# Block-sparse attention and a token/channel mixer: hand-emitted program order against an order made by a list scheduler

## The chip, the cores and the metric

The kernel runs on one core of one Trainium2 chip. The metric is the time of one execution on the device, in microseconds (us). Lower is better. The engines are named as in the profile: PE is TensorE, DVE is VectorE, ACT is ScalarE, POOL is GpSimd, SP is SyncE.

## What is computed

Attention over 4 batches of 8 heads, 768 positions and 64 elements a head, with a mask made of blocks of 32, and behind it a mixer over tokens and channels. Cut to what matters:

```python
scores = q @ k.transpose(0, 1, 3, 2) / np.sqrt(D)      # (4, 8, 768, 768)
mask = band of blocks | first and last block row and column | 3 sampled blocks per block row
attn = softmax(np.where(mask, scores, -1e9))
x = (attn @ v).transpose(0, 2, 1, 3).reshape(4, 768, 512)
h = np.maximum(x.transpose(0, 2, 1) @ w_tok1, 0.0) @ w_tok2   # 768 -> 256 -> 768
u = x + h.transpose(0, 2, 1)
out = u + np.maximum(u @ w_ch1, 0.0) @ w_ch2                  # 512 -> 1536 -> 512
```

## The kernel before

Work goes head by head, 32 slots in all. For a slot, `load_qkv` (L132 to L134) loads q, k and v through POOL's queue, position p of each block of 128 on partition p, so that every partition gets six separate runs of 64 elements. `emit_transposes` turns the six blocks of q (L188) and of k (L196) on PE, one head at a time, and DVE copies the results (L193, L201) into `qtb` and `ktb`. These have 24 more rows, which hold the mask in a form that the score matmul adds by itself: `indf` says to which block a position belongs, `e2sb` which blocks are forbidden. They are built at the start on POOL, DVE and PE (L82 to L174) and put in place by four loads within SBUF (L177, L178).

`attention` then goes through six blocks of 128 keys, called steps here. A step makes the scores of 128 keys against 768 queries (L214 with 512 columns, L218 with 256) in one of two `ps` buffers; ACT takes the exp of all 768 into `et` (L222); six matmuls of 65 columns (L224, called PV here) add into `po`, whose 65th column collects the sums. After six steps DVE takes the reciprocals (L232) and scales the six blocks into `x` (L234).

`make_mixer_groups` cuts the mixer of a batch into 38 groups: two for the first token matmuls (`g_tok1`, L249), six for the second, the addition of x and the transposes of u (`g_tok2`, L268, L276, L279, L284), 24 for the first channel matmuls and their relu (`g_ch1`, L296, relu on DVE at L302), six for the second and the output (`g_ch2`, L313, L320, L321). They share two psum buffers `pm`.

The order of every engine comes from the order in which the code calls these functions, and from priorities: transposes, scores and the scaling stand in `high_priority` blocks, PV and mixer behind them. The groups of a batch are handed out over the seven slots that follow it by `PACING`; the last batch's groups come when all slots are done.

Of the kernel before, what the change touches and what calls it, by code (L numbers as in the profile page):

```python
# [23 lines left out]


@with_exitstack
def kernel(
# [12 lines left out]
    nc = tc.nc  # L40
# [5 lines left out]
    NSLOT = B * H  # L46
    MASKVAL = -30000.0
    NSRC = 4
# [5 lines left out]
    psM = ctx.enter_context(tc.tile_pool(name="psM", bufs=2, space=bass.MemoryType.PSUM))  # L54

    qsrc = [sb1.tile([128, NC, 64], BF16, name=f"qsrc{n}") for n in range(NSRC)]
    ksrc = [sb1.tile([128, NC, 64], BF16, name=f"ksrc{n}") for n in range(NSRC)]
    vaug = [sb1.tile([128, NC, 65], BF16, name=f"vaug{n}") for n in range(NSRC)]

    qtb = [sb1.tile([128, S], BF16, name=f"qtb{i}") for i in range(2)]  # L60
    ktb = [sb1.tile([128, S], BF16, name=f"ktb{i}") for i in range(2)]

    w_tok1 = sb1.tile([128, 6, 256], BF16, name="w_tok1")
    w_tok2 = sb1.tile([128, 2, 768], BF16, name="w_tok2")
    w_ch1 = sb1.tile([128, 4, 1536], BF16, name="w_ch1")
    w_ch2 = sb1.tile([128, 12, 512], BF16, name="w_ch2")

    ident = sb1.tile([128, 128], BF16, name="ident")

    samp64 = sb1.tile([24, 3], I64, name="samp64")  # L70
    sampf = sb1.tile([24, 6], FP32, name="sampf")
    kbi = sb1.tile([24, 24], I32, name="kbi")
    kbf = sb1.tile([24, 24], FP32, name="kbf")
    eq0 = sb1.tile([24, 24], FP32, name="eq0")
    eq1 = sb1.tile([24, 24], FP32, name="eq1")
    allow = sb1.tile([24, 24], FP32, name="allow")
    bandg = sb1.tile([24, 24], FP32, name="bandg")
    t2add = sb1.tile([24, 24], BF16, name="t2add")
    indf = sb1.tile([24, S], BF16, name="indf")
    e2sb = sb1.tile([24, S], BF16, name="e2sb")  # L80

    nc.gpsimd.memset(ident[:, :], 1.0)  # L82
# [4 lines left out]
    nc.gpsimd.iota(kbi[:, :], pattern=[[1, 24]], base=0, channel_multiplier=0)  # L87
    nc.gpsimd.memset(bandg[:, :], 1.0)
    nc.gpsimd.affine_select(
        out=bandg[:, :], in_=bandg[:, :], compare_op=ALU.is_ge, fill=0.0,  # L90
        base=1, pattern=[[1, 24]], channel_multiplier=-1,
    )
    nc.gpsimd.affine_select(
        out=bandg[:, :], in_=bandg[:, :], compare_op=ALU.is_ge, fill=0.0,
        base=1, pattern=[[-1, 24]], channel_multiplier=1,
    )
    nc.gpsimd.affine_select(
        out=bandg[:, :], in_=bandg[:, :], compare_op=ALU.is_ge, fill=1.0,
        base=-1, pattern=[[0, 24]], channel_multiplier=1,
    )  # L100
# [12 lines left out]
    nc.gpsimd.memset(indf[:, :], 1.0)
    nc.gpsimd.affine_select(
        out=indf[:, :], in_=indf[:, :], compare_op=ALU.is_ge, fill=0.0,
        base=0, pattern=[[1, S]], channel_multiplier=-32,
    )
    nc.gpsimd.affine_select(
        out=indf[:, :], in_=indf[:, :], compare_op=ALU.is_ge, fill=0.0,
        base=31, pattern=[[-1, S]], channel_multiplier=32,  # L120
    )

    def qkv_src_ap(t: bass.AP, b: int, h: int) -> bass.AP:
        off = (b * H + h) * S * D
        return APx(t, off, [[D, 128], [128 * D, NC], [1, D]])

    def load_qkv(slot):
        if slot >= NSLOT:
            return
        b, h = slot // H, slot % H  # L130
        n = slot % NSRC
        nc.gpsimd.dma_start(out=ksrc[n][:, :, :], in_=qkv_src_ap(k, b, h))  # L132
        nc.gpsimd.dma_start(out=qsrc[n][:, :, :], in_=qkv_src_ap(q, b, h))  # L133
        nc.gpsimd.dma_start(out=vaug[n][:, :, 0:64], in_=qkv_src_ap(v, b, h))  # L134

    load_qkv(0)
# [42 lines left out]
    for n in range(NSRC):  # L179
        nc.vector.memset(vaug[n][:, :, 64:65], 1.0)  # L180
# [221 lines left out]
```

## Time and profile before

| what | before |
|---|---|
| time, median of 3 runs | 361.43 us (360.75 to 367.4) |
| profiled execution, span | 362.9 us |
| PE busy | 325.2 us, 90% |
| DVE busy | 182.1 us, 50% |
| ACT busy | 142.1 us, 39% |
| POOL busy | 89.7 us, 25% |
| chain that ended last | PE 76%, ACT 8%, DMA 8%, POOL 3%, DVE 2% |

The profile is of one execution. Its span, from the first to the last instruction, is 1.5 us above the median of the runs, 0.4%; the profile shows no time outside the span. A matmul's duration in the profile goes to the end of its last result, and matmuls overlap in the engine, so that the spacing of starts in a run without gaps says what one costs. The granted clock is given as a share of TensorE's full 2.4 GHz: 1.00 is 2.4 GHz, 0.50 is 1.2 GHz, and values between are means over a stretch.

### The profile page before, as it was taken

To read this page: it belongs to the slowest core of one execution; us is meant where nothing else is said; L and a number is where in the kernel's file an instruction comes from. 1 tells how busy PE (TensorE), PEld (TensorE's weight loads), DVE (VectorE), ACT (ScalarE), POOL (GpSimd) and SP (SyncE) were. 2 spreads that over 40 slices of the span, in tenths; PEclk is the share of its full clock that TensorE was granted. 3 is DMA by queue.
4 is the path that set the end of the run, shared out by engine and by line. 5 is a ranking of instruction groups with operands and counts; after the bars stand their busy time and mean duration, and the time that the engine had idled before them with its cause. 6 is when DMAs were issued, how large, how long until landed. Compare 5 with 4: busy or idle time off the path is not lost.

```text
span 362.9 us, 6617 instructions
## 1 busy us (share of the span) xinstructions
PE 325.2 (90%) x2786; PEld 183.3 (51%) x2786; DVE 182.1 (50%) x478; ACT 142.1 (39%) x193; POOL 89.7 (25%) x123
## 2 busy tenths in 40 slices
PE   0795688899899999999999999999999999679995
PEld 0453356565556555455555555455555555235542
DVE  3331243436768633356667544347676534546722
ACT  1293467775622334465604333385404440000000
POOL 9954543524310222233210222220000000000000
PEclk9997599999999999999999999999999999859999
DMA  5999959688641455559531565651101012000022
GB/s 40 136 198 194 153 37 67 46 54 53 41 29 8 28 62 85 84 61 60 33 23 11 34 88 84 75 51 12 13 0 13 2 58 98 21 0 2 0 85 90
DMA packets 82162, 20.24 MB, mean 56 GB/s; under 512 B 75892, under 2 KB 78548, under 8 KB 82132
## 3 DMA queue, kind: packets, MB, share of 16 engines
q0 software_dynamic: 78496, 13.38, 47.3%
q1 hardware_dynamic: 3636, 6.44, 4.7%
q8 instruction: 22, 0.36, 0.4%
q14 instruction: 8, 0.07, 0.1%
HBM read 26.74 MB, written 6.29 MB: 91 GB/s over the span
## 4 chain that ended last, share of the span: by engine, by line
PE 76%; ACT 8%; DMA 8%; POOL 3%; DVE 2%; issue 2%; ACTq 0%; POOLq 0%
PE pm_ch L296 19%; PE pm_ch L313 16%; PE ps L214 13%; PE po L224 10%; ACT et L222 8%; PE ps L218 5%; PE tk L196 4%; DMA w_ch<-in_moe_w_ch_dram 3%; PE pm_tok L249 3%; PE tq L188 3%; PE pm_tok L268 3%; DMA qsrc<-in_q_dram 3%; DMA w_tok<-in_moe_w_tok_dram 2%; PE pm_ut L279 2%; DVE u L276 1%
## 5 line engine op out<-in xcount | busy, mean ns | idle before, releaser
L222 ACT ACTIVATE et<-ps 128x768 bf16<-128x768 f32 x192 | 140.8, 814 | 155.2 <-PE po L224 132.6
L214 PE MATMUL ps<-qtb,ktb 88*128 88x512 bf16 x192 | 76.3, 397 | 7.8 <-ACT et L222 6.4
L296 PE MATMUL pm_ch<-uT,w_ch 128*128 128x384 bf16 x384 | 75.0, 332 | 0.0
L313 PE MATMUL pm_ch<-w_ch,rc 128*128 128x512 bf16 x288 | 71.4, 379 | 0.0
L302 DVE TENSOR_SCALAR rc<-pm_ch 128x384 bf16<-128x384 f32 x96 | 53.1, 556 | 18.3 <-PE pm_ch L296 14.3
L224 PEld LDWEIGHTS <-et 128*128 128x128 bf16 x1152 | 50.7, 100 | 18.0 <-issue 2.8
L224 PE MATMUL po<-vaug,et 128*128 128x65 bf16 x1152 | 58.2, 196 | 0.0
L218 PE MATMUL ps<-qtb,ktb 88*128 88x256 bf16 x192 | 54.2, 282 | 0.0
L132 POOL DMA_DIRECT2D ksrc<-in_k_dram x32 | 26.7, 833 | 96.1 <-PE tk L196 86.0
L296 PEld LDWEIGHTS <-w_ch 128*128 128x128 bf16 x384 | 36.7, 99 | 27.1 <-issue 4.2
L193 DVE COPY qtb<-tq 64x768 bf16<-64x768 bf16 x32 | 17.6, 549 | 61.3 <-PE ps L218 59.7
L134 POOL DMA_DIRECT2D vaug<-in_v_dram x32 | 26.5, 829 | 77.6 <-PE po L224 74.3
L313 PEld LDWEIGHTS <-rc 128*128 128x128 bf16 x288 | 26.5, 97 | 27.5
L234 DVE TENSOR_SCALAR x<-po,recip 128x64 bf16<-128x64 f32 x192 | 39.7, 276 | 1.0
L320 DVE TENSOR_TENSOR o<-pm_ch,u 128x512 f32<-128x512 f32 x24 | 16.5, 687 | 38.7 <-PE pm_ch L313 38.7
L201 DVE COPY ktb<-tk 64x768 bf16<-64x768 bf16 x32 | 17.6, 549 | 34.6 <-PE tk L196 32.5
L218 PEld LDWEIGHTS <-ktb 88*128 88x128 bf16 x192 | 19.0, 99 | 27.3 <-issue 19.3
L133 POOL DMA_DIRECT2D qsrc<-in_q_dram x32 | 26.6, 831 | 8.5 <-PE tq L188 7.8
L214 PEld LDWEIGHTS <-ktb 88*128 88x128 bf16 x192 | 19.0, 99 | 14.1 <-issue 2.8
L188 PE MATMUL tq<-ident,qsrc 128*64 128x128 bf16 x192 | 18.3, 236 | 7.6 <-DMA qsrc<-in_q_dram 5.9
L196 PE MATMUL tk<-ident,ksrc 128*64 128x128 bf16 x192 | 23.0, 234 | 1.1 <-DVE qtb L193 1.1
L196 PEld LDWEIGHTS <-ksrc 128*64 128x64 bf16 x192 | 13.5, 113 | 18.3 <-issue 17.3
(48 smaller groups left out, 127.5 us busy)
## 6 DMA issues: line engine op xcount, KB each, us to landing
out_dram<-o SPq DMA_DIRECT2D x24, 256.0 KB, 2.3
ksrc<-in_k_dram POOLq DMA_DIRECT2D x32, 96.0 KB, 3.1
qsrc<-in_q_dram POOLq DMA_DIRECT2D x32, 96.0 KB, 3.4
vaug<-in_v_dram POOLq DMA_DIRECT2D x32, 96.0 KB, 3.1
w_ch<-in_moe_w_ch_dram POOLq DMA_DIRECT2D x8, 384.0 KB, 11.1
w_tok<-in_moe_w_tok_dram POOLq DMA_DIRECT2D x2, 384.0 KB, 7.3
ktb<-indf SPq DMA_DIRECT2D x2, 36.0 KB
qtb<-e2sb SPq DMA_DIRECT2D x2, 36.0 KB
```

What stands on the lines that cost most here:

```text
L132: nc.gpsimd.dma_start(out=ksrc[n][:, :, :], in_=qkv_src_ap(k, b, h))
L133: nc.gpsimd.dma_start(out=qsrc[n][:, :, :], in_=qkv_src_ap(q, b, h))
L188: nc.tensor.matmul(out=tq[:, 128 * c : 128 * c + 128], lhsT=qsrc[n][:, c, :], rhs=ident[:, :], start=(c == 0), stop=(c == NC - 1), is_tran ...
L196: nc.tensor.matmul(out=tk[:, 128 * c : 128 * c + 128], lhsT=ksrc[n][:, c, :], rhs=ident[:, :], start=(c == 0), stop=(c == NC - 1), is_tran ...
L214: nc.tensor.matmul(out=ps[:, 0:512], lhsT=kt[0:88, 128 * j : 128 * j + 128], rhs=qt[0:88, 0:512], start=True, stop=True,)
L218: nc.tensor.matmul(out=ps[:, 512:768], lhsT=kt[0:88, 128 * j : 128 * j + 128], rhs=qt[0:88, 512:768], start=True, stop=True,)
L222: nc.scalar.activation(out=et[:, j, :], in_=ps[:, :], func=AF.Exp, scale=0.125)
L224: nc.tensor.matmul(out=po[:, c, :], lhsT=et[:, j, 128 * c : 128 * c + 128], rhs=vaug[n][:, j, :], start=(j == 0 and c == 0), stop=(j == NC ...
L234: nc.vector.tensor_scalar(out=x_tiles[c][:, 64 * h : 64 * h + 64], in0=po[:, c, 0:64], scalar1=recip[:, c : c + 1], scalar2=None, op0=ALU. ...
L296: nc.tensor.matmul(out=pm[:, 0:384], lhsT=w_ch1[:, dmc, 128 * cc : 128 * cc + 128], rhs=st["uT"][:, dmc, 384 * sh : 384 * sh + 384], start ...
L302: nc.vector.tensor_scalar(out=rc[:, cc, 384 * sh : 384 * sh + 384], in0=pm[:, 0:384], scalar1=0.0, scalar2=None, op0=ALU.max,)
L313: nc.tensor.matmul(out=pm[:, :], lhsT=rc[:, cc, 128 * sc : 128 * sc + 128], rhs=w_ch2[:, cc, :], start=(cc == 0), stop=(cc == 11),)
```

## The change

The program is written anew. What it does:

- **Order.** The context is told to keep the order as emitted. A class `Planner` walks through a model of time while the program is traced. PE has five streams with fixed ranks: scores, PV, transposes of q and k, token mixer, channel mixer. At each moment of the model the first stream whose next matmul is ready is emitted. ACT and DVE take ready work from a list by rank; exps are ACT's first rank, and ACT takes a copy or a relu only when no exp is outstanding. Whatever may run on either is offered to ACT first.
- **Pairs of heads.** Loads, transposes and steps go by pairs. A transpose turns 128x128, both heads at once. A step covers half the queries of two heads: two score matmuls of 384 columns, one exp of 768, six PV.
- **Six rows per partition.** Partition p holds positions 6p to 6p+5, so that a load has runs of 384 elements. A copy on DVE lays k and q out for the transposes (L349), and one puts v into `vaug` (L346). The weights `w_tok1`, `w_tok2` and the output follow the same order of rows; `w_tok2` is laid out once by a copy (L655).
- **Mask rows.** They are made in partitions 64 to 87 and copied within them by DVE and ACT, without loads.
- **Mixer.** The token mixer goes by half batches (256 columns); u is written over x. DVE scales a half pair in one operation (L485). Relus and the copies of transposed tiles may run on ACT. Three psum buffers serve transposes and mixer; there are two `rc` buffers.
- **Channel mixer last.** As the lowest stream it gets what the others leave.

The diff, cut to its core:

```diff
+    def step(self):
+        if self.free_at["pe"] <= self.now:
+            for s in self.streams:
+...
+                if t <= self.now:
+                    s[3] = None
+                    emit()
+                    self.free_at["pe"] = self.now + cost
+...
+        for eng in ("act", "dve"):
+...
+                if eng == "act" and prio > 0 and self.exp_pending:
+                    continue
+...
-    psM = ctx.enter_context(tc.tile_pool(name="psM", bufs=2, space=bass.MemoryType.PSUM))
+    psM = ctx.enter_context(tc.tile_pool(name="psM", bufs=3, space=bass.MemoryType.PSUM))
+    ctx.enter_context(tc.manual_schedule())
...
-        return APx(t, off, [[D, 128], [128 * D, NC], [1, D]])
+                in_=APx(src, 2 * p * S * D, [[NC * D, 128], [S * D, 2], [1, NC * D]]),
...
-    for i in range(2):
-        nc.sync.dma_start(out=qtb[i][64:88, :], in_=e2sb[:, :])
-        nc.sync.dma_start(out=ktb[i][64:88, :], in_=indf[:, :])
+    for n in range(2):
+        nc.vector.tensor_copy(out=ktb[n][R, :], in_=indf)
+    for n in range(2):
+        nc.scalar.copy(
+            out=qtb[n][R, :].rearrange("k (h s) -> k h s", h=2), in_=pm[R, :, 0:384]
+        )
...
+                nc.vector.tensor_copy(
+                    out=lay[:, :, :, :], in_=raw[:, :, :, :].rearrange("p h c d -> p c h d")
+                )
...
+                        lhsT=lays[nm][:, c, :, :].rearrange("p h d -> p (h d)"),
+                        rhs=ident[:, :], start=(c == 0), stop=(c == NC - 1), is_transpose=True,
...
+                for hd in range(2):
+                    n = 2 * (p % NV) + hd
+                    nc.tensor.matmul(
+                        out=ps[:, hd, 0:384], lhsT=ktb[n][0:88, 128 * j : 128 * j + 128],
+                        rhs=qtb[n][0:88, 384 * half : 384 * half + 384], start=True, stop=True,
+                    )
...
+                ev = P.op(("act",), {"act": 735.0}, [done], exp, prio=0, lat=80.0)
...
+                ev = P.op(("dve",), {"dve": 760.0}, [done], norm, prio=1)
...
+        return P.op(("dve", "act"), {"dve": dve_psum(n), "act": act_cost(n)}, deps, emit, prio=prio)
...
-    PACING = [(0, 8), (8, 16), (16, 24), (24, 32), (32, 34), (34, 36), (36, 38)]
+    P.stream(0, qk_stream())
+    P.stream(1, pv_stream())
+    P.stream(2, tr_stream())
+    P.stream(3, tok_stream())
+    P.stream(4, ch_stream())
```

Three places in the orders. The first is POOL's start. `kbi`, `bandg`, `indf` and `ind` belong to the mask, `ksrc`, `qsrc` and `kraw`, `qraw` are the loads of k and q. Before, from its first instruction in the kernel:

```order
L82 MEMSET ident 128x128
L87 IOTA kbi 24x24
L83 AFFINE_SELECT ident<-ident 128x128
L88 MEMSET bandg 24x24
L113 MEMSET indf 24x768
L89 AFFINE_SELECT bandg<-bandg 24x24
L132 DMA ksrc_74<-in_k_dram 128x6x64
L93 AFFINE_SELECT bandg<-bandg 24x24
L114 AFFINE_SELECT indf<-indf 24x768
L97 AFFINE_SELECT bandg<-bandg 24x24
L133 DMA qsrc_70<-in_q_dram 128x6x64
```

Now, from the same place to the first load of v:

```order
L225 DMA kraw_100<-in_k_dram 128x2x384
L225 DMA qraw_102<-in_q_dram 128x2x384
L244 AFFINE_SELECT ident<-ident 128x128
L248 IOTA kbi 24x24
L249 AFFINE_SELECT ind<-ind 24x768
L253 AFFINE_SELECT ind<-ind 24x768
L261 AFFINE_SELECT bandg<-bandg 24x24 x6
L225 DMA vraw_128<-in_v_dram 128x2x384
```

The loads of k and q moved ahead of the mask's work, the load of v behind it, and the three memsets went to DVE.

The second is PE inside attention, while a mixer is being fed in (`ps` scores, `tk` a transpose of k, `po` PV, `pm_tok` token mixer). Before, in slot 8; of rows that repeat one stands:

```order
L249 LDWEIGHTS w_tok_86
L249 MATMUL pm_tok_0_0_994<-x_5_200,w_tok_86 128x512
L214 LDWEIGHTS ktb_84
L214 MATMUL ps_2_1256<-qtb_82,ktb_84 128x512
L218 LDWEIGHTS ktb_84
L218 MATMUL ps_2_1256<-qtb_82,ktb_84 128x256
L249 MATMUL pm_tok_0_1_1002<-x_0_195,w_tok_86 128x512
L214 MATMUL ps_3_1266<-qtb_82,ktb_84 128x512
L218 MATMUL ps_3_1266<-qtb_82,ktb_84 128x256
L249 MATMUL pm_tok_0_1_1002<-x_1_196,w_tok_86 128x512
```

Now, in the fifth pair's first steps; of rows that repeat one stands:

```order
L470 LDWEIGHTS et_1_4_946
L470 MATMUL po_1_919<-vaug_81,et_1_4_946 128x65
L553 LDWEIGHTS w_tok_74
L553 MATMUL pm_tok_0_0_1_948<-a_t_0_808,w_tok_74 128x256
L375 LDWEIGHTS klay_973
L375 MATMUL tk_986<-ident,klay_973 128x128
L424 LDWEIGHTS ktb_90
L424 MATMUL ps_0_1_989<-qtb_82,ktb_90 128x384
L424 LDWEIGHTS ktb_91
L424 MATMUL ps_0_1_989<-qtb_83,ktb_91 128x384
L470 LDWEIGHTS et_1_5_967
L470 MATMUL po_1_919<-vaug_81,et_1_5_967 128x65
```

Between two pairs of score matmuls there stand the six PV of two steps earlier and one to four short matmuls of transposes or token mixer; before, PV of a slot came in lumps and mixer matmuls of 512 columns one at a time.

The third is PE at the end of attention (`pm_ch` channel mixer, `pm_tok` token mixer, `pm_ut` transposes of u). Before, after the last PV; of rows that repeat one stands:

```order
L249 LDWEIGHTS w_tok_86
L249 MATMUL pm_tok_3_0_4003<-x_0_3003,w_tok_86 128x512
L249 MATMUL pm_tok_3_1_4011<-x_5_3008,w_tok_86 128x512
L268 LDWEIGHTS w_tok_87
L268 MATMUL pm_tok_3_0_4020<-a_t_4002,w_tok_87 128x512
L279 LDWEIGHTS u_0_4023
L279 MATMUL pm_ut_0_4025<-ident,u_0_4023 128x128
L268 MATMUL pm_tok_3_1_4031<-a_t_4002,w_tok_87 128x512
```

Now, from the last score matmul on; of rows that repeat one stands:

```order
L424 MATMUL ps_1_5_3234<-qtb_89,ktb_97 128x384
L470 MATMUL po_1_3203<-vaug_81,et_1_3_3216 128x65
L614 MATMUL pm_ch_0_2_1_3232<-uT_1155,w_ch_75 128x384
L470 MATMUL po_1_3203<-vaug_81,et_1_5_3245 128x65
L614 MATMUL pm_ch_0_3_0_3255<-uT_1155,w_ch_75 128x384
L528 MATMUL pm_tok_3_1_3278<-x_2638,w_tok_72 128x256
L614 MATMUL pm_ch_0_4_0_3276<-uT_1155,w_ch_75 128x384
L553 MATMUL pm_tok_3_1_0_3302<-a_t_1_3292,w_tok_74 128x256
L614 MATMUL pm_ch_0_4_1_3297<-uT_1155,w_ch_75 128x384
```

The last batch's token mixer stood alone before; now it stands among channel matmuls of the first batch, and the channel mixers of all four batches follow.

## Rows read from the trace of the kernel before

**Rows 1.** The page: span, then busy time, share and instructions of each engine.

```profile
span 362.9 us, 6617 instructions
...
PE 325.2 (90%) x2786; PEld 183.3 (51%) x2786; DVE 182.1 (50%) x478; ACT 142.1 (39%) x193; POOL 89.7 (25%) x123
```

**Rows 2.** Timeline, runs of PE: start us, us, what, xcount.

```profile
53.20 0.50 PE L188 MATMUL tq<-ident,qsrc 128*64 128x128 bf16 x6 [0.26 <-DVE ktb L201]
...
104.29 1.15 PE L296 MATMUL pm_ch<-uT,w_ch 128*128 128x384 bf16 x6
...
300.27 1.27 PE L224 MATMUL po<-vaug,et 128*128 128x65 bf16 x36
...
308.42 2.75 PE L249 MATMUL pm_tok<-x,w_tok 128*128 128x512 bf16 x12 [0.61 <-DVE x L234]
...
343.40 15.70 PE L313 MATMUL pm_ch<-w_ch,rc 128*128 128x512 bf16 x72
```

**Rows 3.** Groups, PE, 280 to 300 us: count, busy us, mean ns, idle before.

```profile
L313 PE MATMUL pm_ch<-w_ch,rc 128*128 128x512 bf16 x47 | 12.1, 379 | 0.0
L214 PE MATMUL ps<-qtb,ktb 88*128 88x512 bf16 x11 | 4.2, 378 | 0.2
L296 PE MATMUL pm_ch<-uT,w_ch 128*128 128x384 bf16 x19 | 3.6, 325 | 0.0
L218 PE MATMUL ps<-qtb,ktb 88*128 88x256 bf16 x11 | 3.0, 270 | 0.0
L224 PE MATMUL po<-vaug,et 128*128 128x65 bf16 x66 | 2.7, 193 | 0.0
```

**Rows 4.** Timeline, the start.

```profile
1.44 0.73 POOL L113 MEMSET indf<- 24x768 bf16 x1
...
6.30 0.84 POOL L134 DMA_DIRECT2D vaug<-in_v_dram  x1
...
7.15 0.22 POOL L109 TENSOR_SCALAR_AFFINE_SELECT bandg<-bandg 24x24 f32<-24x24 f32 x1
...
7.61 0.52 DVE L162 TENSOR_SCALAR t2add<-allow 24x24 bf16<-24x24 f32 x1
...
10.21 0.94 DVE L174 CAST e2sb<-ps_e 24x768 bf16<-24x768 f32 x1
...
14.38 0.58 PE L214 MATMUL ps<-qtb,ktb 88*128 88x512 bf16 x1 [0.37 <-DMA qtb<-e2sb]
...
17.49 0.62 PE L214 MATMUL ps<-qtb,ktb 88*128 88x512 bf16 x1
...
20.41 0.62 PE L214 MATMUL ps<-qtb,ktb 88*128 88x512 bf16 x1
```

**Rows 5.** Windows: stretch, length, busy us of PE, PEld, DVE, ACT, POOL; clock; DMA; GB/s.

```profile
14.40:40.00 25.60, 19.86 (x150) 10.87 (x149) 6.53 (x22) 15.86 (x21) 14.70 (x21) 0.83 1.42 188
...
60.00:80.00 20.00, 18.07 (x215) 11.84 (x213) 8.17 (x30) 15.84 (x23) 8.85 (x11) 1.00 0.93 60
...
280.00:300.00 20.00, 19.81 (x157) 10.70 (x156) 8.29 (x23) 8.83 (x12) 0.00 (x0) 1.00 0.10 38
...
310.00:330.00 20.00, 14.72 (x65) 6.42 (x64) 10.64 (x19) 0.00 (x0) 0.00 (x0) 0.66 0.00 0
```

**Rows 6.** Timeline, PE at 32 us.

```profile
31.96 0.85 PE L188 MATMUL tq<-ident,qsrc 128*64 128x128 bf16 x6 [3.95 <-DMA qsrc<-in_q_dram]
```

**Rows 7.** Timeline, ACT and PE at 53 us, attention alone.

```profile
53.04 4.33 ACT L222 ACTIVATE et<-ps 128x768 bf16<-128x768 f32 x6 [1.34 <-PE po L224]
...
54.60 0.38 PE L214 MATMUL ps<-qtb,ktb 88*128 88x512 bf16 x1 [0.22 <-ACT et L222]
```

**Rows 8.** Groups, whole span.

```profile
L222 ACT ACTIVATE et<-ps 128x768 bf16<-128x768 f32 x192 | 140.8, 814 | 155.2 <-PE po L224 132.6 <-PE ps L218 22.5
...
L193 DVE COPY qtb<-tq 64x768 bf16<-64x768 bf16 x32 | 17.6, 549 | 61.3 <-PE ps L218 59.7 <-PE tq L188 1.6
...
L276 DVE TENSOR_TENSOR u<-pm_tok,x 128x512 bf16<-128x512 f32 x24 | 16.5, 686 | 2.2 <-PE pm_tok L268 2.2
```

More of the change, by code (lines that the diff above doesn't have):

```diff
@@ L73 @@
[L73 to L82, printed above, removed]
+    psM = ctx.enter_context(tc.tile_pool(name="psM", bufs=3, space=bass.MemoryType.PSUM))
@@ new lines @@
+    ch_there = Ev(48.0 * US)
+    sampf = sb1.tile([128, 6], FP32, name="sampf")
+    kbf = sb1.tile([128, 24], FP32, name="kbf")
+    eq0 = sb1.tile([128, 24], FP32, name="eq0")
+    eq1 = sb1.tile([128, 24], FP32, name="eq1")
+    allow = sb1.tile([128, 24], FP32, name="allow")
+    t2add = sb1.tile([128, 24], BF16, name="t2add")
+    for n in range(NV):
+        nc.vector.memset(vaug[n][:, :, :, 64:66], 1.0)
+    nc.vector.tensor_copy(out=kbf[R, :], in_=kbi[R, :])
+    nc.vector.tensor_copy(out=sampf[R, :], in_=samp64[R, :].bitcast(I32))
@@ new lines, in wtok2_lay, with tr_stream, tok_stream, ch_stream @@
+    def wtok2_lay(eng):
+        nc.vector.tensor_copy(
+            out=w_tok2[:, :, :, :],
+            in_=w_tok2r[:, :, :].rearrange("t k (p c) -> t k c p", c=NC),
+        )
+    for p in range(NP):
+        for h in range(2):
+            x_there[p, h] = Ev()
+    def tr_stream():
+        for p in range(NP):
+            yield from transposes(p)
+    def tok_stream():
+        for b in range(B):
+            for g in range(2):
+                yield from tok(b, g)
+    def ch_stream():
+        for b in range(B):
+            yield from ch(b, psM, "pm")
@@ new lines @@
+    P.stream(0, qk_stream())
[3 more added lines that the diff above has]
+    P.stream(4, ch_stream())
+    for n in range(2, 2 * NV):
+        more_mask_rows(n)
+    tok2_op = P.op(("dve",), {"dve": 900.0}, [Ev(20.0 * US)], wtok2_lay, prio=4)
+    loaded = 4
+    ch2_loaded = False
+    while P.streams or P.ops:
+        while loaded < NP and kT_there.get((loaded - NR, 0)) is not None and all(
+            e.t is not None for e in (qT_there[loaded - NR, 1], va_there[loaded - NR])
+        ):
+            load_pair(loaded, P.now + 6.0 * US)
+            loaded += 1
+            if not ch2_loaded:
+                ch2_loaded = True
+                for i in range(4):
+                    nc.gpsimd.dma_start(
+                        out=w_ch2[:, 3 * i : 3 * i + 3, :],
+                        in_=APx(moe_w_ch2, i * 3 * 128 * DM, [[DM, 128], [128 * DM, 3], [1, DM]]),
+                    )
+        assert P.step(), ("stuck", P.now, len(P.streams), len(P.ops))
@@ L375 @@
+    if PLAN:
+        print("plan", P.now)
 _INS = ['q', 'k', 'v', 'sampled_blocks', 'moe_w_tok1', 'moe_w_tok2', 'moe_w_ch1', 'moe_w_ch2']
```

721 lines of the change are left out of this document (461 added, 260 removed).

## The prediction

> **What bounds the kernel now.** I read the busy shares first. TensorE (PE) is busy for 325.2 of 362.9 us, 90% [rows 1], and the reader should distrust that figure. A matmul's row runs until its modelled end, so a busy PE may still be waiting. I therefore asked for the spacing of matmuls in runs without a gap [rows 2]: the last minus its own length, over the number of steps. 72 matmuls of 512 columns take 15.70 us: (15.70 - 0.38)/71 = 0.216 each. 384 columns: (1.15 - 0.325)/5 = 0.165. The 12 of 512 columns in L249 also give 0.216, so 0.108 for 256 columns. PV (65 columns): (1.27 - 0.193)/35 = 0.0309. A 128-column transpose: (0.50 - 0.22)/5 = 0.0555. (A single one lasts 0.38, 0.325 and 0.193 [rows 3]; 0.22 is my estimate for a transpose, between PV's 0.193 and L218's 0.270.) At these prices all matmuls of this kernel are about 272 us of work; the other 91 us lie in four places.
>
> The start: the first score matmul runs at 14.38 [rows 4]. A starved stretch: in 14.4 to 40 us PE is busy 19.86 of 25.60 at a granted clock of 0.83, because a transpose waited 3.95 us for its query load [rows 5, 6]. The tail: in 310 to 330 us PE is busy 14.72 of 20 at 0.66, the last batch's token mixing alternating with VectorE (DVE), nothing else left to run [rows 5]. And in between a score matmul waits about 0.2 us on the exp when attention runs by itself [rows 7]: exps of 0.81 then follow each other by (4.33 - 0.81)/5 = 0.704 us, the pace of ScalarE (ACT) [rows 7, 8].
>
> **The change as an absolute sum.** Every stage of the new kernel is priced by itself, against the profiled execution's span of 362.9; the median of the runs shown, 361.43, is 1.5 less, and I take that off at the end.
>
> *Start.* The last small select on POOL ends at 7.37 now [rows 4]. The v load (0.84) goes behind it and the big memset (0.73) to DVE, so it ends at about 5.8. The two DVE steps to the mask need 0.73 more (7.40 to 8.13), the two mask matmuls 1.0: 7.5. The mask rows no longer go through SBUF-to-SBUF loads; ACT copies them twice. ACT has no such row; DVE's cast of 24x768 took 0.94 [rows 4], so 9.4, and between 8 and 9.4 if it is faster. DVE meanwhile makes two row copies, two relayouts, two more row copies and two evacuations of 768 elements, 8 x 0.549 [rows 8], from 6.5: 10.9. First score matmul at **11.0** (9.5 if the SBUF copies are cheap, 14.4 if the double-sized first loads land late).
>
> *Attention.* 192 steps of two 384-column score matmuls (2 x 0.165) and six PV (0.185), as before; the pair transposes halve the transposes, 384 to 192 (10.7 us of PE gone). Between the first and the last score matmul the new PE order holds 384 score, 1134 PV, 180 transposes, 168 token-mixing matmuls of 256 columns, 84 u transposes and 21 ch1: 63.4 + 35.0 + 10.0 + 18.1 + 4.7 + 3.5 = 134.7 us. ACT's floor is 192 x 0.704 = 135.2, so the two engines are level, step by step. With two score buffers and exp (0.81) plus score matmuls (0.33 and 0.2 to the end) per buffer, two steps take about 1.4 us, just twice 0.70. There is no slack: a step with more than 0.705 of PE work is late by the difference, and a shorter one does not win it back. Counted over the 191 steps in the new order, 116 are over 0.705 by 7.6 us in all; the sum of the larger of the two is 142.3. Mixed streams do not run at the clean spacing: in 280 to 300 us the rows make 47 x 0.216 + 11 x 0.216 + 19 x 0.165 + 11 x 0.108 + 66 x 0.0309, with three transposes 19.1 us of work, for 19.81 busy [rows 3, 5], so 4% more. With 1.04 on PE's part the sum is 146.5. At first TensorE runs at 1.2 GHz (a 512-column matmul lasts 0.62 there and 0.38 later), and steps take (20.41 - 17.49)/3 = 0.97 [rows 4, 7]; that held from 14.38 to about 21, so 7 steps x 0.27 = 2. Attention **148.5** (bounds 137, ACT alone, and 170, rival B).
>
> What this rests on: DVE keeps up. In that stretch it has 32 norms, 62 evacuations, 48 relayout copies, 21 u additions, 14 uT copies, 7 a_t and 6 relus. The relayout copy (768 elements bf16, SBUF to SBUF) has no row; the nearest is the 768-element copy of L193, 0.549, the dear end is the 0.94 cast, the cheap end nothing. With 0.549 for copies and L276's 0.686 for the rest (a norm with its reciprocal too) [rows 4, 8]: 110 x 0.549 + 14 x 0.549 + 66 x 0.686 = 113 of 148 us, 77%; with 0.94 for the 48, 132. I take 0.549 and no loss.
> The Trainium skill (VectorE: DVE Perf Modes, section "What auto-detection actually checks") says that a single-source 16-bit copy within SBUF can take a mode of four elements a cycle; by its formula the copy would be an estimated 0.36 us and DVE's load 104. No row here shows it, and the sum above does not change by it.
>
> Loads: up to the first weights for ch1 the new order moves 4.7 MB (four pairs of q, k, v, 2.36; token weights 0.79; w_ch1 1.57). At the 188 GB/s of 14.4 to 40 us [rows 5] that is 25 us, while pair 3 is wanted after three pairs of 12 steps, at about 38 us. So the 3.95 us wait [rows 6] and its slow clock go, covered by some 10 us; without that cover it costs 4 to 6. POOL's issues (48 instead of 96 for q, k, v) stay off the path.
>
> *Behind attention.* 363 ch1, 288 ch2, 18 PV, 24 token mixing, 12 u transposes are left: 59.9 + 62.2 + 0.6 + 2.6 + 0.7 = **126.0**. The last token mixing lies among ch1 matmuls of older batches, so the 310 to 330 stretch has no successor. Nearly all relus run on ACT now, one per group of four ch1 (0.66). No row shows ACT on 384 elements: between nothing and the 0.704 of 768. At the dear end 85 x 0.045 = 4 us more; I take none. With three instead of two psum buffers the ch1 groups should run at 0.165.
>
> *End.* PE's last matmul ends at 343.40 + 15.70 = 359.1, the span at 362.9 [rows 1, 2]: **3.8**, unchanged.
>
> Sum: 11.0 + 148.5 + 126.0 + 3.8 = 289.3, less 1.5: **288 us**, 0.80 of before.
>
> **Rivals.** *C, ACT's floor.* The steps run at ACT's pace throughout, the long ones absorbed, no mixing loss: 135.2 + 2 for attention, 277 us. For it speaks that exps ran at 0.704 in attention alone [rows 7]; against it the 116 long steps and the 4%.
>
> *B, DVE's queue.* An evacuation stands behind an addition or norm (0.686) on DVE's fixed order, PE stands behind it, with its score matmuls queued. There are 32 transposed tiles: 22 us if each is late by one such op and PE has nothing else; I price three in four, 17 us: 305. DVE at 77% speaks for it, the deep prefetch of pairs against it.
>
> *D, slower than before: the clock falls in attention.* PE waits for the exp in every short step, and TensorE stays at 1.2 GHz. Here it went to 0.66 in 310 to 330 us when PE alternated with DVE [rows 5]. At half clock the 134.7 us become 269: 11 + 269 + 126 + 4 - 1.5 = 408. It is slower than before by 2% (over 368.7) when attention takes 229, that is when two thirds of it are spent slow. Against it: in 60 to 80 us, attention with the same gaps, the clock was 1.00 [rows 5], and at half clock PE has no gaps left.
> The Trainium skill (TensorE: Matmul & The Clock Gate, section "A second HAM failure mode: psum-queue depth-cycling") tells of such short idles between groups of matmuls making the clock swing; the 310 to 330 row agrees, the 60 to 80 row does not.
>
> **How the numbers follow.** 288 gets 0.63 (its own range 278 to 299), B 0.20, C 0.12, D 0.03; 0.02 are for a B so bad that it ends near 361. Range 275 to 308. About 2% is what a measurement of this kernel can tell from no change: faster 0.95, same 0.02, slower 0.03.
>
> **What would show it.** First score matmul near 11; last exp near 159; granted clock 1.00 from about 18 us; exps 0.75 to 0.78 apart in the mean; 72 ch2 in 15.6 us, ch1 at 0.165. If the waits of PE in attention name DVE evacuations, it is B; if the last exp comes before 150, C. An attention over 190 us, or a tail over 135, would make the prediction wrong.

## The result, and the profile after

The changed kernel takes **293.53 us** (median of 4 runs, 293.13 to 294.31), against 362.91 for the kernel before, timed beside it. The ratio is 0.811 (95% interval 0.807 to 0.816). Forecast was 288 us, with a range of 275 to 308. The profiled execution took 294.31 us with a span of 292.5, so 1.8 us lie outside the span. Each of the four runs has that difference (1.8 to 1.9 us), and the kernel before, where time and span of one run are both known, has 1.7 to 1.8: it has time outside the span too.

The page of the changed kernel, span and busy times (answers to [rows 1]), and its chain of work that ended last:

```profile
span 292.5 us, 6359 instructions
...
PE 273.3 (93%) x2690; PEld 178.4 (61%) x2690; DVE 129.1 (44%) x281; ACT 193.2 (66%) x289; POOL 45.2 (15%) x72
...
PE 64%; ACT 24%; DMA 4%; DVE 2%; issue 2%; POOL 2%; POOLq 0%; ACTq 0%
```

PE's busy time fell by 52 us and its share rose only from 90 to 93%. Priced at the clean spacings, all matmuls come to some 271 us before and 262 now, so that only 10 of the 52 us are matmuls that went. The other 42 lay inside busy rows, beyond the price of the matmuls: that excess was 54 us and is 12. DVE lost 53 us and ACT took over the relus. DMA's share of the chain is halved and not gone, 4%.

The timeline of PE: the first and the last score matmul, and two runs without a gap behind attention (answers to [rows 2] and, for the start, [rows 4]).

```profile
11.73 0.48 PE L424 MATMUL ps<-qtb,ktb 88*128 88x384 bf16 x1 [1.95 <-DVE qtb L393]
...
162.23 0.49 PE L424 MATMUL ps<-qtb,ktb 88*128 88x384 bf16 x2
...
194.82 15.76 PE L614 MATMUL pm_ch<-uT,w_ch 128*128 128x384 bf16 x96
210.42 15.70 PE L636 MATMUL pm_ch<-w_ch,rc 128*128 128x512 bf16 x72
...
272.70 15.70 PE L636 MATMUL pm_ch<-w_ch,rc 128*128 128x512 bf16 x72
```

So the span splits into a start of 11.7, an attention of 150.7 (11.73 to 162.4, when the last score matmul has started), 126.0 of mixer behind it, to the end of the last matmul at 272.70 + 15.70 = 288.4, and an end of 4.1. The last row is the one that answers to the tail of before: no token mixing is left there. 96 ch1 matmuls in a row are (15.76 - 0.326)/95 = 0.162 apart.

Stretches of the changed kernel (length, then busy us of PE, PEld, DVE, ACT, POOL with instructions, granted clock, DMA share, GB/s), answering to [rows 5]:

```profile
13.00:30.00 17.00, 15.80 (x174) 10.73 (x172) 10.13 (x26) 15.10 (x21) 9.71 (x14) 1.00 1.17 204
30.00:50.00 20.00, 17.10 (x217) 12.87 (x215) 13.79 (x33) 15.29 (x21) 10.23 (x15) 0.84 1.27 203
...
60.00:160.00 100.00, 99.05 (x1407) 76.14 (x1405) 65.53 (x143) 99.60 (x135) 9.30 (x13) 1.00 0.22 31
```

In 60 to 160 us the clock is 1.00 and 135 exps run, one each 0.74 us. The stretch from 30 to 50 us stands out: 0.84, PE busy 17.10 of 20. The timeline there (POOL, DVE, PE and ACT, other rows left out) shows why:

```profile
39.84 0.71 POOL L225 DMA_DIRECT2D vraw<-in_v_dram  x1 [1.20 <-DMA w_ch<-in_moe_w_ch_dram]
...
44.14 0.36 DVE L349 COPY klay<-kraw 128x768 bf16<-128x768 bf16 x1 [2.95 <-DMA kraw<-in_k_dram]
...
44.55 0.61 PE L375 MATMUL tk<-ident,klay 128*128 128x128 bf16 x4 [2.63 <-DVE klay L349]
...
44.95 0.85 PE L424 MATMUL ps<-qtb,ktb 88*128 88x384 bf16 x2
...
45.90 0.81 ACT L432 ACTIVATE et<-ps 128x768 bf16<-128x768 f32 x1 [3.25 <-PE ps L424]
```

One pair's k arrives 2.95 us late; the copy, the transposes, the scores and the exps wait in turn. The k is that of pair 5 (pairs count from 0), landed at 44.11. The score matmuls at 44.95 belong to pair 3, whose own k landed at 22.4: they need nothing from this load and wait only because pair 5's transposes stand ahead of them in PE's order. It is the successor of the 3.95 us wait of [rows 6], at another place. POOL itself waits for loads of `w_ch`: the weights stand in the same queue.

### The profile page after: what moved, and what is told of

Same layout as the page of the kernel before. It is cut to its first block, busy times and chain, and to the rows that moved or that the text cites. A ratio compares the mean times of both kernels' runs of the same rounds, so it can differ in the third digit from the quotient of the medians.

```text
span 292.5 us, 6359 instructions
## 1 busy us (share of the span) xinstructions
PE 273.3 (93%) x2690; PEld 178.4 (61%) x2690; DVE 129.1 (44%) x281; ACT 193.2 (66%) x289; POOL 45.2 (15%) x72
## 4 chain that ended last, share of the span: by engine, by line
PE 64%; ACT 24%; DMA 4%; DVE 2%; issue 2%; POOL 2%; POOLq 0%; ACTq 0%
ACT et L432 23%; PE pm_ch L636 21%; PE pm_ch L614 21%; PE ps L424 10%; PE po L470 5%; DMA kraw<-in_k_dram 4%; PE pm_tok L528 2%; PE pm_tok L553 2%; PE pm_ut L578 1%; PE tk L375 1%; PE tq L375 1%; DVE qtb L393 1%; DVE ktb L393 1%; ACT qtb L314 1%; POOL bandg L261 0%
## 5 line engine op out<-in xcount | busy, mean ns | idle before, releaser
L424 PE MATMUL ps<-qtb,ktb 88*128 88x384 bf16 x384 | 97.9, 337 | 4.6 <-DVE qtb L393 2.0
L510 ACT ACTIVATE rc<-pm_ch 128x384 bf16<-128x384 f32 x90 | 44.1, 490 | 63.3 <-PE pm_ch L614 47.2
L644 DVE TENSOR_TENSOR o<-pm_ch,x 128x512 f32<-128x512 f32 x24 | 16.6, 691 | 101.6 <-PE pm_ch L636 101.6
L561 DVE TENSOR_TENSOR x<-pm_tok,x 128x512 bf16<-128x512 f32 x24 | 16.3, 688 | 7.8 <-PE pm_tok L553 7.5
L485 DVE TENSOR_TENSOR x<-po,recip 128x384 bf16<-128x384 f32 x32 | 17.8, 557 | 1.1
L528 PE MATMUL pm_tok<-x,w_tok 128*128 128x256 bf16 x96 | 17.3, 272 | 0.0
L553 PE MATMUL pm_tok<-a_t,w_tok 128*128 128x256 bf16 x96 | 16.8, 272 | 0.2 <-DVE x L561 0.2
L225 POOL DMA_DIRECT2D vraw<-in_v_dram x16 | 11.5, 721 | 29.1 <-DVE vaug L346 26.8
L225 POOL DMA_DIRECT2D kraw<-in_k_dram x16 | 12.3, 769 | 7.2 <-DVE qlay L349 1.8
L225 POOL DMA_DIRECT2D qraw<-in_q_dram x16 | 11.6, 723 | 5.1 <-DVE vaug L346 1.9
## 6 DMA issues: line engine op xcount, KB each, us to landing
w_ch<-in_moe_w_ch_dram POOLq DMA_DIRECT2D x8, 384.0 KB, 11.9
```

The source lines that it names most:

```text
L225: nc.gpsimd.dma_start(out=raw[:, :, :, :], in_=APx(src, 2 * p * S * D, [[NC * D, 128], [S * D, 2], [1, NC * D]]),)
L424: nc.tensor.matmul(out=ps[:, hd, 0:384], lhsT=ktb[n][0:88, 128 * j : 128 * j + 128], rhs=qtb[n][0:88, 384 * half : 384 * half + 384], star ...
L485: nc.vector.tensor_tensor(out=free(xs[b][:, 3 * half, 128 * pb : 128 * pb + 128], 0, [[64, 2], [DM, 3], [1, 64]]), in0=po[:, :, :, 0:64], ...
L510: nc.scalar.activation(out=o(), in_=i, func=AF.Relu)
L528: nc.tensor.matmul(out=box["pm"][:, t, :], lhsT=w_tok1[:, sc, 128 * t : 128 * t + 128], rhs=xs[b][:, sc, 256 * g : 256 * g + 256], start=( ...
L553: nc.tensor.matmul(out=ubox["pm"][:, i, :], lhsT=w_tok2[:, t, 2 * s2 + i, :], rhs=a_t[:, t, :], start=(i == 0 and t == 0), stop=(i == 1 an ...
```

## The experiments

Each is an edit of the changed kernel. "Attention" is from the start of the first to the start of the last score matmul, "behind" from there to the end of the span. A time is of two executions unless the row says otherwise, and attention and behind are of one. The rows come from three rounds, in which the kernel before was timed and the changed kernel was not, so that differences of about 1 us between rows are not told from none.

| kernel | time, us | attention | behind |
|---|---|---|---|
| the changed kernel | 293.53 (4 runs) | 150.7 | 130.1 |
| w_ch2 loaded last | 289.31 (4 runs) | 145.6 | 130.1 |
| token mixer after attention | 326.36 (one run) | 148.0 | 164.9 |
| mixer ahead of attention | 304.31 (one run) | 247.2 | 43.4 |
| single transposes | 318.19 | 169.8 | 135.1 |
| pair transposes twice | 301.47 | 152.0 | 137.2 |
| single transposes in blocks of six | 308.50 | 159.6 | 135.9 |
| k, q loaded in short runs | 301.09 | 156.1 | 130.1 |
| relayout copies twice | 300.70 | 157.4 | 130.1 |
| the same, planned with their price | 297.00 | 151.4 | 133.2 |
| two psum buffers | 304.47 | 149.2 | 142.6 |
| w_ch2 last, start evacuated on DVE | 288.82 (4 runs) | 146.1 | 130.1 |
| the same, exps planned at 0.705 | 290.25 (4 runs) | 144.4 | 133.0 |

**The loads.** Four loads of w_ch2 (1.57 MB) are issued between pair 4 and pair 5. They are moved behind the last pair:

```diff
-            if not ch2_loaded:
+            if not ch2_loaded and loaded == NP:
```

> The four loads of w_ch2 are issued behind the last pair's loads instead of between pair 4 and pair 5. Theory (POOL's queue): pair 5's load of k came 2.95 us late because the w_ch2 loads stood ahead of it, and the clock fell to 1.2 GHz in that wait; without them the wait goes, attention shrinks from 150.7 to about 146 us and the time by 4 to 6 us, to 287.5 to 289.5. Rival (bandwidth): the loads run at about 203 GB/s from 13 to 60 us whatever their order, the wait only moves to another pair, and the time stays within 1 us of 293.5.

Measured: 289.31 us (289.18 to 289.41), 4.2 less. The stretch of the wait in this kernel:

```profile
30.00:50.00 20.00, 19.63 (x291) 15.17 (x289) 17.48 (x42) 19.88 (x28) 11.01 (x15) 1.00 1.30 201
```

28 exps instead of 21 and a clock of 1.00, at the same 201 GB/s: not more bandwidth, only another order. Attention is 5.1 us shorter, all of it from here. This version beats both kernels; its ratio to before is 0.799 (0.791 to 0.807). The same edit is in the last two rows of the table, with 0.799 (0.793 to 0.804) and 0.800 (0.794 to 0.806).

**Where the mixer lies.** First, the token mixer may not start before the last exp:

```diff
         deps = [x_there[2 * g + 4 * b + i, h] for i in range(2) for h in range(2)] + [tok_there]
+        deps.append(et_there[steps[-1]])
```

> The token mixers wait for the last exp, so that attention runs without filler. Theory (a step takes the larger of ACT's 0.705 and PE's work): attention falls from 150.7 to about 143 us (136 by the sum, 2 for the slow start, 5 for the late load), what is behind it grows from 126 to 152.5 and a little for the token chain at its head; 311 to 318 us in all. Rival (attention is paced by something else, DVE or the loop over two score buffers): attention stays at 149 to 151, the time goes to 320 or more.

Measured 326.36: above the theory and in the rival's range; attention itself, 148.0, lies between the two. It does not end much sooner although a fifth of PE's work left it (108 us instead of 134, at the prediction's prices), and the work comes back behind: 164.9 instead of 130.1. Its stretch of 60 to 160 us, and the one just behind attention:

```profile
60.00:160.00 100.00, 90.41 (x1198) 60.86 (x1196) 40.77 (x103) 99.79 (x138) 9.32 (x13) 1.00 0.22 30
...
160.00:180.00 20.00, 16.09 (x154) 12.06 (x152) 9.20 (x16) 5.72 (x10) 0.00 (x0) 1.00 0.00 1
```

In the windows' columns the fourth of these counts is ACT's: 138 exps here against 135 in the changed kernel, all that ACT does there. With nearly nothing to mix ACT sets the pace and PE has 10 us free, but exps still come (100.0 / 138) 0.72 apart, not the 0.704 of [rows 7], and the load wait is still there. What keeps the exps from 0.704 here no run tells. Without 5.1 us for the wait this attention would take 142.9 against 145.6: 26 us of PE's mixing work cost attention less than 3 us. Behind, PE is busy only 16.09 of 20: token chains alone cannot fill it, as in the old tail.

Second, the opposite: the mixer's streams rank above the scores.

```diff
-    P.stream(3, tok_stream())
-    P.stream(4, ch_stream())
+    P.stream(-2, tok_stream())
+    P.stream(-1, ch_stream())
```

> The token and channel mixers rank ahead of scores, so that a batch's channel mixer runs as one lump of 31 us as soon as it can, and the last batch's mixer alone at the end. The PE work is the same. Theory (the mixer's place matters as filler beside the exps): the sum of the larger of 0.705 and PE's work per step rises from 142.3 + 126.2 to 248.9 + 35.2, by 15.6 us, and the last token mixer stands alone again, 3 to 8 us; 310 to 318 us. Rival (PE does the same work in any order and is busy all the time): within 3 us of 293.5.

Measured 304.31, under the range. The expectation forgot that the load wait vanishes when attention is slower: no copy waits for k in this run, and against the kernel with the late w_ch2, which has no such wait either, it is 15.0 us more. The token mixer that stands alone at the end did cost what was expected (43.4 behind, 4.1 more than 35.2 of work and 4.1 of end); the rest of the miss is attention, 247.2, where the 248.9 of the sum and 3 us of slow start were to be expected. ACT now waits 58.5 us for scores (7.1 in the changed kernel), and still only 11 us are lost, because PE has other work meanwhile (busy for 92% of the span). What the two runs say together: token mixers held back until after attention cost 33 us, and a mixer that goes first costs 11, or 15 without the load wait. How much of the 69 us the order brings by itself is not shown, since no run has the old order in the new program.

**The pair transposes.** One head at a time again, 64 columns of weights instead of 128, 384 transposes instead of 192:

```diff
-                        lhsT=lays[nm][:, c, :, :].rearrange("p h d -> p (h d)"),
+                        lhsT=lays[nm][:, c, hd, :],
```

> q and k are transposed one head at a time, 384 transposes of 64 columns of weights instead of 192. Theory (PE is the bound, so that all PE work counts): the new order holds 139.8 us between the first and the last score matmul and 130.8 behind it, instead of 134.3 and 126.2; the larger-of-two sum gives 6.7 us more, so 299 to 302 us. Rival (the transposes fill time in which PE would wait for exps): less than 2 us more.

Measured 318.19: both wrong, by far. Behind attention it is as expected; attention is 19 us longer. A wait does not explain it: ACT's waits for scores are 12.6 us in all, none over 0.95, and PE is busy throughout. The timeline of PE does. First the single transposes, then the changed kernel:

```profile
64.73 0.49 PE L425 MATMUL ps<-qtb,ktb 88*128 88x384 bf16 x2
65.06 0.34 PE L471 MATMUL po<-vaug,et 128*128 128x65 bf16 x6
65.34 0.35 PE L378 MATMUL tq<-ident,qlay 128*64 128x128 bf16 x3
65.62 0.50 PE L425 MATMUL ps<-qtb,ktb 88*128 88x384 bf16 x2
```

```profile
64.29 0.34 PE L470 MATMUL po<-vaug,et 128*128 128x65 bf16 x6
64.47 0.27 PE L375 MATMUL tk<-ident,klay 128*128 128x128 bf16 x2
64.58 0.28 PE L375 MATMUL tq<-ident,qlay 128*128 128x128 bf16 x2
```

Read the starts. Six PV take 0.18 until a pair transpose (64.29 to 64.47), and 0.28 until a single one (65.06 to 65.34). Three single transposes take 0.28 until the next score matmul, where 3 x 0.056 = 0.17 is their own work. So PE pays 0.10 us when its weights go from 128 columns to 64, and 0.11 until it is back. Over all 61 visits after 60 us the medians say the same: 0.093 more from a PV to the first transpose, 0.024 on the first when others follow, 0.096 on the last, 0.21 a visit. The run shows 95 visits. Two runs test this against a rival, that the number of transposes does it. In one, every pair transpose is issued twice (the second copy into a part of the tile that is not read):

> Every pair transpose is issued twice, with the planner's price doubled; the second copy goes to a part of the psum tile that nobody reads, so the number of transposes is that of the single ones and their weights keep 128 columns. Theory S (what made the single transposes dear is the change between weights of 128 and of 64 columns: in that run a transpose run before a score matmul lasts 0.12 us longer, and the matmuls ahead of it 0.10 longer, than with pairs): only 180 more transposes at 0.056 = 10 us of PE work, of which the load wait hides up to half: first to last score matmul 155 to 161 us, time 298 to 304. Rival N (it is the number of transposes and of PE instructions that delays the steps): the stretch is near that of the single transposes, 167 to 172, time 312 or more.

In the other, six single transposes of a tile stand together:

> Single-head transposes again, but the six of a tile stand in one block (price 0.55 us in the planner), so that the weights change between 128 and 64 columns 60 times in and out instead of about 108. Theory S: 48 fewer changes at 0.22 us = 10.6 us less than with single transposes set one by one (169.8): first to last score matmul 157 to 162, time 305 to 310. Rival N: no gain from the blocks, 168 or more, time 315 to 320.

Measured: 301.47 and 308.50, both by theory S; its attention lengths were 155 to 161 and 157 to 162, measured 152.0 and 159.6, with 7 and 6 us more mixer left behind, which the lengths had not counted. With 384 transposes of 128 columns the span grows by 8.7 (10 us of work); with 60 visits instead of 95 it is 9.2 shorter than with single transposes, for 35 x 0.21 = 7.4 and a start at a granted clock of 1.00 where the single ones ran at 0.62 in 12 to 30 us. A row of the kernel with blocks:

```profile
75.27 0.52 PE L378 MATMUL tq<-ident,qlay 128*64 128x128 bf16 x6
75.72 0.50 PE L426 MATMUL ps<-qtb,ktb 88*128 88x384 bf16 x2
```

Six take 0.45, that is 6 x 0.056 + 0.12: the price is one per visit and not one per transpose. Added up without the steps, the costs are too dear (10.7 of work plus 20 or 12.6 of visits, less the 5.1 of the load wait, which is gone there: 25.5 and 18.2, where the spans grew by 23.7 and 14.5), because a step with less than 0.705 of PE work hides them. Put into the sum over the steps, with 0.21 a visit, the 176 steps of the single transposes from 29 us on, when the clock is back at 1.00, come to 151.6 us, and 151.0 were measured. What is left of that attention, some 6 us beyond the sum, lies before, under the low clock. With blocks of six the same sum gives 147.7 for 172 steps, where 141.2 were measured. There a step with six transposes stands beside steps with none, and part of a long step seems to be won back by the next, against the prediction's "a shorter one does not win it back"; no run tests this.

The Trainium skill (TensorEngine Tiling (Array Packing), section "Key Properties") says that changing the tiling mode drains TensorE, and counts 128 rows by 64 columns as a mode. The trace agrees, with 0.10 and 0.11 us; the score matmuls, whose weights are 88 by 128, show no such gap (0.029 us from a PV to a score matmul and 0.162 from a score matmul to a PV, as between matmuls of their own kind).

**The relayout.** Two ways at its cost. k and q loaded straight into the order that the transposes want, in runs of 64 elements and by heads, so that DVE's copy is a plain one:

```diff
-            raw = sbw.tile([128, 2, NC, D], BF16, tag=f"{nm}raw", bufs=NR, name=f"{nm}raw{p}")
+            shape = [128, 2, NC, D] if nm == "v" else [128, NC, 2, D]
+                for hd in range(2):
+                    nc.gpsimd.dma_start(
+                        out=raw[:, :, hd, :],
+                        in_=APx(src, (2 * p + hd) * S * D, [[NC * D, 128], [D, NC], [1, D]]),
+                    )
```

> q and k are loaded straight into the layout of the transposes, in runs of 64 elements as in the kernel before, one load for each head (80 loads of q, k, v instead of 48). Theory (the rate of loading, not the length of the runs, was at its limit: 188 GB/s before, 203 after, with six times longer runs): within 2 us of 293.5. Rival (short runs are what starved the kernel before): the loads slow down, further waits for k and q appear in attention before 60 us, and the time rises by 5 us or more.

Measured 301.09, 7.6 more: the rival was right. In 12 to 20 and 20 to 30 us the loads run at 142 and 164 GB/s, where the changed kernel has 192 and 209, and DVE waits for k twice, 8.0 us in all, instead of once, 3.0:

```profile
12.00:20.00 8.00, 5.82 (x39) 3.49 (x40) 6.58 (x16) 5.08 (x7) 8.00 (x11) 1.00 1.37 142
20.00:30.00 10.00, 9.21 (x122) 6.17 (x120) 5.60 (x12) 9.93 (x14) 8.29 (x11) 1.00 1.79 164
```

Two things do it. POOL has two more loads to issue ahead of the mask's work, and the first score matmul comes at 13.57, 1.8 us later. The rest is in attention, 5.4 us, and there it is the transfers: of the loads that POOL had issued 10 us before, those of k and q (96 KB, short runs) land 0.6 to 0.7 us apart from 50.4 us on, and a load of v behind them (192 KB, long runs) takes 1.02. In the changed kernel seven loads of 192 KB land 0.95 to 1.03 apart from 47.4 us on. So the short runs move about 150 GB/s and the long ones 200. The 188 GB/s of the expectation was a mean with the weights' loads in it.

Then all 48 copies of q, k and v are done twice, with the planner's price as it was (0.32), and again with a price of 0.65:

```diff
+                for _ in range(2):
+                    nc.vector.tensor_copy(
+                        out=lay[:, :, :, :], in_=raw[:, :, :, :].rearrange("p h c d -> p c h d")
+                    )
```

> Each of the 48 relayout copies on DVE is done twice, 17 us more of DVE work in attention. Theory (DVE has slack and sets nothing): at most 2 us more. Rival (B of the prediction, PE stands behind DVE's queue): 8 us or more, with waits of score matmuls and transposes on DVE.

> All 48 copies of q, k and v on DVE doubled as before, but the planner now prices them 0.65 instead of 0.32 us. If the 7 us of the first doubling came from an order that was planned with wrong times, they go: first to last score matmul 150 to 153, time 293 to 296. If DVE's work itself delays the steps, they stay: 156 to 159, time 299 to 302.

Measured 300.70 and 297.00. The first lies between its two expectations, and so does the second in time, while its attention, 151.4, is what was expected if the wrong plan did it. In the first ACT waits for scores 24 times, 11.9 us in all; in the second 11 times, 8.4, 3.0 of it the load wait. The second pays its 3.5 us behind attention, where 21 token matmuls more than in the changed kernel were left over. So about half of the 7 us came from an order planned with wrong times, and the other half from token mixing that the plan found no room for beside the doubled copies: DVE takes on 17 us more work, but not for nothing, and a wrong price costs about as much as the work itself when the order is fixed beforehand.

**Three psum buffers.** `psM` and the planner's "pm" set from 3 to 2.

> Two psum buffers instead of three for transposes and mixer. Theory (the third buffer is what brings ch1 from 0.18 to 0.163 per matmul): with ACT's relu of 0.49 the groups of four take about 0.71 instead of 0.65, 5 us more behind attention, and PE waits for evacuations inside attention, 3 to 8 us; 300 to 307 us. Rival (the faster relu on ACT is enough): less than 2 us more.

Measured 304.47: the total as expected, the place not. Attention is no longer; all 12.4 us are behind it. There 60 ch1 in a row run 0.173 apart instead of 0.162 (0.175 in the mean of all), which makes 4 to 5 us; 24 more token matmuls and their transposes were left over, 3 to 4 us; and in 160 to 180 us PE is busy only 17.54 of 20, 2.5 us. These overlap in part, so that 1 to 3 us of the 12.4 stay open.

**Better versions.** On top of the late w_ch2, three of the first pair's four evacuations go to DVE; then, in a further run, the planner's exp is also cut to the pace that the trace shows.

```diff
-                ev = P.op(("dve", "act"), {"dve": 550.0, "act": 740.0}, [last], evac, prio=2)
+                engines = ("dve",) if p == 0 and (nm, hd) != ("q", 1) else ("dve", "act")
+                ev = P.op(engines, {"dve": 550.0, "act": 740.0}, [last], evac, prio=2)
```

> e1, and of the first pair's four evacuations three are on DVE and one on ACT, so that the two halves of the first transposed tile are not read by two engines. Theory: the first score matmul comes 0.8 us earlier (10.9), the time 0.5 to 1 us below e1. Rival (the first pair is bound by ACT's casts anyway): as e1 within 0.3 us.

> The kernel with w_ch2 loaded last and three of the first four evacuations on DVE, and the planner's price of an exp cut from 0.735 to 0.705 us, the pace that the trace shows. Theory: the order changes little, the sum over the steps of the larger of PE's and ACT's work is 141.2: 287.5 to 289.5, the same. Rival: exps were held back by the planner's price; attention is 2 to 4 us shorter, 284.5 to 286.5.

Measured 288.82 (288.25 to 289.52) and 290.25 (290.01 to 290.59). The first is as fast as the late w_ch2 alone, within what can be told: the first score matmul comes at 11.3 instead of 11.7, and attention is 0.5 longer. In the second attention is 1.7 us shorter than in the first and the part behind 2.9 longer: a faster plan for the exps only moved token mixing to the back.

## Why the prediction was right, step by step

The direction and the size came out. 288 (287.8 before rounding) was low by 0.7 from the start, 2.2 from attention, 0.3 from the end and 2.5 from the step from span to time. That attention came so near is luck, since a cost that did not exist stood in for one that was put at nothing.

- **Start**, 11.0 forecast, 11.73 measured. Both prices of copies were too dear: ACT's cast of the mask rows takes 0.74 (bound 0.94) and a relayout copy 0.36 (0.549 taken). Against that POOL's last select ended at 6.89 where 5.8 was forecast, so that the mask matmuls and the casts came later. What was not in the sum: ACT's and DVE's reads of the two halves of one transposed tile came one after the other. The timeline of the start:

```profile
5.30 1.59 POOL L261 TENSOR_SCALAR_AFFINE_SELECT bandg<-bandg 24x24 f32<-24x24 f32 x6
...
8.21 1.48 ACT L314 CAST qtb<-ps_e 24x768 bf16<-24x768 f32 x2 [6.12 <-PE ps_e L307]
...
9.71 0.79 ACT L391 COPY ktb<-tk 64x768 bf16<-64x768 bf16 x1
...
10.54 0.56 DVE L393 COPY ktb<-tk 64x768 bf16<-64x768 bf16 x1 [1.16 <-ACT ktb L391]
...
11.13 0.55 DVE L393 COPY qtb<-tq 64x768 bf16<-64x768 bf16 x1
...
11.71 0.80 ACT L391 COPY qtb<-tq 64x768 bf16<-64x768 bf16 x1 [1.21 <-DVE qtb L393]
```

- **Attention**, 148.5 forecast, 150.7 measured. The forecast was 142.3 for the sum over the steps, 4.2 for mixed streams and 2 for the slow start. The runs show 142.3, about nothing for mixing, 3.0 for the slow start, 5.1 for the load wait, and 0.2 because the measured length goes one score matmul further.
  - *The load wait.* The step that failed is "So the 3.95 us wait [rows 6] and its slow clock go, covered by some 10 us". Without the wait attention takes 145.6, so the wait cost 5.1, inside the 4 to 6 that the prediction gave for a lost cover. The count of 4.7 MB was for the loads up to ch1's weights; it did not list w_ch2, which the new code issues between pairs 4 and 5. The queue then held 1.57 MB ahead of pair 5, some 8 us at the 203 GB/s of that stretch. And the cover was counted to the wrong moment: pair 3, which it was counted for, had all its loads by 24.4 us, but in the new order PE wants pair 5's k right behind the first step of pair 3, at 41.8 us.
  - *The slow start.* The first eight steps, 11.73 to 20.48, took 8.74 us, where the sum over the steps has 5.76. A score matmul lasts 0.48 to 0.53 until 19.7 us and 0.32 after it, which is TensorE at 1.2 and at 2.4 GHz; the clock column of the row from 13 us on reads 1.00 all the same. Steps without transposes took 0.94 to 0.97 as forecast, but three steps held the transposes of pair 1 and took 1.2 to 1.5, and the first two took 1.1:

```profile
14.88 0.83 PE L424 MATMUL ps<-qtb,ktb 88*128 88x384 bf16 x2
...
15.85 0.83 PE L424 MATMUL ps<-qtb,ktb 88*128 88x384 bf16 x2
...
17.33 0.85 PE L424 MATMUL ps<-qtb,ktb 88*128 88x384 bf16 x2
...
18.73 0.84 PE L424 MATMUL ps<-qtb,ktb 88*128 88x384 bf16 x2
...
19.93 0.49 PE L424 MATMUL ps<-qtb,ktb 88*128 88x384 bf16 x2
```

  - *Mixed streams.* In the kernel with the late w_ch2 the 183 steps behind the slow start take 136.7 us, where the sum of the larger of PE's and ACT's work has 136.5. So the sum was right without the 4%, which was read from one window of before and does not carry over. Of the 0.7 us that this window lacked, one visit to 64-column weights (its three transposes) takes 0.2; the rest stays open.
- **DVE keeps up.** Its instructions in attention add up to 108 of 150.7 us, 72%, where 77% was forecast (67% when overlaps count once), with the copies at 0.354 to 0.361 in the mean:

```profile
L346 DVE COPY vaug<-vraw 128x768 bf16<-128x768 bf16 x16 | 5.7, 354 | 0.9 <-DMA vraw<-in_v_dram 0.9
L349 DVE COPY qlay<-qraw 128x768 bf16<-128x768 bf16 x15 | 5.4, 361 | 0.6 <-DMA qraw<-in_q_dram 0.6
L349 DVE COPY klay<-kraw 128x768 bf16<-128x768 bf16 x15 | 5.4, 360 | 3.0 <-DMA kraw<-in_k_dram 3.0
```

  With the cycles that the Trainium skill (VectorE: DVE Perf Modes, section "Side-by-side: where the cycles go for N=2048 bf16") counts for a copy at four elements a cycle, such a copy is an estimated 0.36 us, and the trace agrees. No loss was taken for DVE and none shows, but the runs with doubled copies, 3.5 and 7.2 us slower, show that its idle share is not all to be had.
- **Behind attention**, 126.0 forecast, 126.0 measured, with the leftover list to the instruction (363 ch1, 288 ch2, 12 and 12 token matmuls, 12 transposes), as the new program's order has it. ch1 at 0.162, ch2 72 in 15.70. Relus of 384 on ACT took 0.490, less than the 0.65 of the four ch1 beside them, and with three psum buffers they hide.
- **End**, 3.8 forecast, 4.1 measured.
- **From span to time**, -1.5 forecast, +1.0 measured (293.53 against 292.5), 2.5 of the 5.5 us missed. The prediction compared one execution's span with the median of other executions. The single run's own time is what should have been used: every run of the new kernel takes 1.8 to 1.9 us more than its span.
- **The rivals.** C (277 us, ACT's floor) did not come: exps were 0.74 apart and not 0.704, which is what the sum over the steps has (142.3 over 191 steps, 0.745). The long steps were not absorbed: in the kernel with the late w_ch2 the 87 steps of more than 0.705 from 60 us on took 67.5 us, priced at 67.6. B, DVE's queue, did not come: in attention PE's idle time names DVE in the load wait alone (2.63). D, the fallen clock, came in the load wait (0.84 in 30 to 50 us) and, by the length of the score matmuls, in the slow start; elsewhere in attention the clock was 1.00.
- **One part was right for too small a reason.** "10.7 us of PE gone" for the pair transposes counts matmuls only. The old kernel goes to 64-column weights 92 times; the same gaps stand in its timeline, PE at 63 us:

```profile
62.83 0.19 PE L224 MATMUL po<-vaug,et 128*128 128x65 bf16 x1
62.95 0.47 PE L196 MATMUL tk<-ident,ksrc 128*64 128x128 bf16 x5
63.35 0.39 PE L214 MATMUL ps<-qtb,ktb 88*128 88x512 bf16 x1
```

One PV takes 0.12 where 0.031 is its price, five transposes 0.40 where 0.28 is theirs: 0.21 a visit, about 19 us in all. So an estimated 30 us of the 69 won are the pair transposes (undoing them in the new kernel cost 24.7 us, or 28.9 against the version without the load wait), and of the "other 91 us in four places" 19 lay in a fifth place, inside PE's busy time. The absolute sum did not need it, since the new kernel has no such visits; a sum of savings would have been 19 us wrong.

## What to carry to other kernels

When PE is the bound, price the new program in absolute terms at the spacing of clean runs, and check the spacing at each change of shape too: a busy engine hides 0.2 us a visit. Count every load that a queue carries ahead of the one that is needed, in the order of issue and up to the last weights; here 1.57 MB in the wrong place cost 5 us, and moving them cost nothing. In a fixed order a load is wanted when its first user's turn comes, and all that stands behind that user waits with it, whether it needs the load or not. With an order fixed beforehand, work that leaves one stage appears in another, so judge an edit by the whole span and never by the length of a stage.

## What was not expected of the hardware

- A change of the weights from 128 to 64 columns and back costs PE 0.10 and 0.11 us, whether three or six transposes lie between.
- Loads of 96 KB in runs of 64 elements landed 0.6 to 0.7 us apart, loads of 192 KB in runs of 384 elements 0.95 to 1.03: some 150 against 200 GB/s.
- ACT and DVE did not read the two halves (partitions 0 to 63 and 64 to 127) of one psum tile together: 1.16 and 1.21 us of waiting at the start. Whether the chip or the waits placed by the tools make this order, no run tells. The Trainium skill (PSUM — Partial Sum Buffer, section "PSUM bank collisions raise a hardware error ⚠️") says that reads of one bank by two engines are kept apart where they touch the same quarter of the partitions; these halves share none, so the page alone would not ask for it.
